# Attention with head mixing and an expert layer on one core: plain float32 products in place of hi/lo splits, and steps of two mixing blocks

## The chip, the core and the metric

One core of one Trainium2 chip runs the whole kernel in one launch. The metric is the device time of an execution in microseconds (us); lower is better. The core's engines are TensorE (PE, with its weight loads listed apart as PEld), VectorE (DVE), ScalarE (ACT), GpSimd (POOL) and SyncE (SP, which here only issues DMAs).

## What is computed

The inputs are `q`, `k`, `v` of shape (8, 12, 448, 64), that is batch, heads, positions and head size, two 12x12 head-mixing matrices and the weights of 8 experts. All are float32.

```python
scores = (1/8) * q @ k.T                                   # per batch and head: 448 x 448
scores = einsum('bhij,hg->bgij', scores, w_pre)            # first mixing, over heads
attn   = exp(scores - max); attn /= sum(attn) + 1e-9       # over keys j
attn   = einsum('bhij,hg->bgij', attn, w_post)             # second mixing, over heads
x      = (attn @ v) laid out as 3584 tokens x 768
expert = argmax(x @ w_gate); gate = softmax weight of it
out    = gate * (relu(x @ w1[expert]) @ w2[expert])
```

## The kernel before

**Tiles and blocks.** For each batch the 448 queries are cut into four tiles `T` of 120, 120, 120 and 88 queries, 32 tiles in all. A tile is cut into *blocks* of 10 queries; 10 queries x 12 heads fill 120 partitions, so both mixings are matrix products with a block-diagonal 120x120 matrix. There are 12 blocks in a tile of 120 queries and 9 in one of 88: 360 blocks.

**The work of a tile and of a block.** `qk(T, h)` (L196 to L210) makes the scores of one head into a PSUM bank `bs`; ACT copies them to `si` (L208), queries on partitions. `relayout` (L212) is a DMA on SP's queue that brings the rows of one block from `si` to `sb`, with (query, head) on partitions. `split` (L218) makes two float32r numbers of each element on DVE: `sh` by a cast (L223) and the rest `sl` by a subtraction (L224). `mix` (L227) is three float32r products WH·sh + WL·sh + WH·sl into a PSUM bank `bm` (L231 to L233), then the row maximum on DVE (L235), the exponential with its row sum on ACT (L237), two small DVE instructions for the reciprocal (L239, L241), and on DVE the second mixing's matrix scaled by it, `wp` (L243). `post` (L247) is the second mixing: four float32 products, one for each 112 keys, that take the exponentials `et` as weights, so the result comes out with keys on partitions (`bp`, L256); ACT copies it to `pt` (L258). `av` (L263, one pair of heads) is the product with `v` in float32: the even head writes PSUM partitions 0 to 63 and the odd head 64 to 127 (L271). `rows` (L289) turns the tile and adds the expert logits; `dispatch` ranks the tokens and scatters them from POOL's queue (L334).

**Splits of q and k.** A float32r score product has K = 128: partitions 0 to 63 hold the high part of `q` and 64 to 127 the rest. It is multiplied with the high part of `k` (`ka`, L203) and with its rest (`kb`, L204); `k` and `q` are each loaded twice, once per half of the partitions (L89, L109), and split by ACT (L96, L116) and DVE (L97, L117) in float32r.

**Order.** The lists of steps (the loop after `PL, QLEAD, RLEAD, SLEAD = 3, 17, 5, 2`) name what is recorded in step `u`, one step per block: the mix of block `u`, one head's scores of a later tile, the relayout of block `u + 5`, the split of block `u + 2`, an `av` pair, the second mixing of block `u - 3`. A scheduler turns these into a fixed instruction order per engine; from then on each engine runs its list in order. Buffers come from pools: two for `si`, four for `sb`, two raw ones and six pairs of halves for `k`, and one for `v`, whose next batch is loaded by the last `av` of a batch. The experts (L427 on) start when the last tile's tokens are dispatched.

Of the kernel before, what the change touches and what calls it, by code (L numbers as in the profile page):

```python
# [38 lines left out]
def attn_moe_kernel(ctx, tc, qT, kT, v, w_pre, w_post, w_gate, w1, w2, out):  # L39
# [32 lines left out]
    bank_s = [ps_s.tile([P, 512], F32, name=f"bs{n}") for n in range(2)]  # L72
    bank_m = [ps_m.tile([IT, 512], F32, name=f"bm{n}") for n in range(2)]
    bank_p = [ps_p.tile([JC, 512], F32, name=f"bp{n}") for n in range(2)]
    bank_a = ps_a.tile([P, 3, IT], F32, name="ba")
    bank_x = [ps_x.tile([P, 512], F32, name="bx"), bank_s[0]]
    turn = {"s": 0, "m": 0, "p": 0}

    def bank(k, banks):
        turn[k] += 1  # L80
        return banks[turn[k] % len(banks)]

    KK, QQ, VV, SI, SB, SH, EE, PT, XT, KR = ({} for _ in range(10))

    def dma_k(b, c, pool):
        raw = pool.tile([P, KC, S], F32, name="kraw")
        src = kT[b, c * KC:(c + 1) * KC].rearrange("h d j -> d h j")
        for half in range(2):
            nc.sync.dma_start(out=raw[half * D:(half + 1) * D], in_=src)  # L89
        KR[b, c] = raw  # L90

    def split_k(b, c, eng=None):
        raw = KR.pop((b, c))
        ka = k_p.tile([P, KC, S], F32R, name="ka")
        kb = k_p.tile([P, KC, S], F32R, name="kb")
        nc.scalar.copy(out=ka, in_=raw)  # L96
        (eng or nc.vector).tensor_sub(out=kb, in0=raw, in1=ka.bitcast(F32))  # L97
        KK[b, c] = (ka, kb)

    def load_k(b, c):  # L100
        dma_k(b, c, kraw_p)
        split_k(b, c)

    def dma_q(T):
        b, it, ni, _ = geom[T]
        raw = q_p.tile([P, H, IT], F32, name="qraw")
        src = qT[b, :, H * it * IT:H * (it * IT + ni)].rearrange("d (h i) -> d h i", h=H)
        for half in range(2):
            nc.sync.dma_start(out=raw[half * D:(half + 1) * D, :, :ni], in_=src)  # L109
        KR[T] = raw  # L110

    def split_q(T):
        b, it, ni, _ = geom[T]
        raw = KR.pop(T)
        qs = q_p.tile([P, H, IT], F32R, name="qs", bufs=2)
        nc.scalar.copy(out=qs[:, :, :ni], in_=raw[:, :, :ni])  # L116
        nc.vector.tensor_sub(out=qs[D:P, :, :ni], in0=raw[D:P, :, :ni],  # L117
                             in1=qs[D:P, :, :ni].bitcast(F32))
        QQ[T] = qs

    def load_q(T):
        dma_q(T)
        split_q(T)

    def load_v(b):
        vt = v_p.tile([JC, NJ, HD], F32, name="vt")
        nc.sync.dma_start(out=vt, in_=v[b].rearrange("(c p) f -> p c f", p=JC))
        VV[b] = vt

    w12 = const.tile([IT, 2, H], F32, name="w12")  # L130
    for n, w in enumerate((w_pre, w_post)):
        nc.scalar.dma_start(out=w12[:, n, :], in_=w.unsqueeze(0).to_broadcast([IB, H, H]))
# [3 lines left out]
    first = ExitStack()  # L136
    first_p = first.enter_context(tc.tile_pool(name="kfirst", bufs=H // KC))
    dma_q(0)
    for c in range(H // KC):
        dma_k(0, c, first_p)  # L140

# [4 lines left out]
    # mask[p, i] = 1 where p // 12 == i  # L146
    mask = const.tile([IT, IB], F32, name="mask")
    nc.gpsimd.memset(mask, 1.0)
    nc.gpsimd.affine_select(out=mask, in_=mask, pattern=[[-H, IB]], compare_op=ALU.is_ge,
                            fill=0.0, base=0, channel_multiplier=1)  # L150
    nc.gpsimd.affine_select(out=mask, in_=mask, pattern=[[H, IB]], compare_op=ALU.is_ge,
                            fill=0.0, base=H - 1, channel_multiplier=-1)
    Wraw = const.tile([IT, IB, H], F32, name="Wraw")
    WH = const.tile([IT, IT], F32R, name="WH")
    WL = const.tile([IT, IT], F32R, name="WL")
    Wpost = const.tile([IT, H, IB], F32, name="Wpost")
    # SCALE is a power of two: exact
    nc.vector.scalar_tensor_tensor(out=Wraw, in0=w12[:, 0:1, :].to_broadcast([IT, IB, H]),
                                   scalar=SCALE, in1=mask.unsqueeze(2).to_broadcast([IT, IB, H]),
                                   op0=ALU.mult, op1=ALU.mult)  # L160
    nc.vector.tensor_tensor(out=Wpost, in0=w12[:, 1, :].unsqueeze(2).to_broadcast([IT, H, IB]),
                            in1=mask.unsqueeze(1).to_broadcast([IT, H, IB]), op=ALU.mult)
    Wraw = Wraw.rearrange("p i g -> p (i g)")
# [8 lines left out]
    tri = const.tile([P, P], BF16, name="tri")      # tri[m, n] = 1 where m < n  # L172
# [14 lines left out]
    # rows that no token has taken: a token id out of range, gate 0  # L187
# [8 lines left out]
    def qk(T, h):  # L196
        b, it, ni, _ = geom[T]
        if h == 0:
# [6 lines left out]
        if T == 0 and h % 3 == 2:  # L205
            nc.vector.tensor_copy(out=SI[T][:ni, h, :], in_=ps[:ni, :S])
        else:
            nc.scalar.copy(out=SI[T][:ni, h, :], in_=ps[:ni, :S])  # L208
        if it == 3 and b + 1 < B and h % KC == KC - 1:
            load_k(b + 1, h // KC)  # L210

    def relayout(T, s):  # L212
        nb = geom[T][3][s]
        sb = sb_p.tile([IT, S], F32, name="sb")
        nc.sync.dma_start(out=sb[:nb * H], in_=SI[T][s * IB:s * IB + nb])
        SB[T, s] = sb

    def split(T, s):  # L218
        R = geom[T][3][s] * H
        sb = SB.pop((T, s))  # L220
        sh = sh_p.tile([IT, S], F32R, name="sh")
        sl = sh_p.tile([IT, S], F32R, name="sl")
        nc.vector.tensor_copy(out=sh[:R], in_=sb[:R])  # L223
        nc.vector.tensor_sub(out=sl[:R], in0=sb[:R], in1=sh[:R].bitcast(F32))  # L224
        SH[T, s] = (sh, sl)

    def mix(T, s):  # L227
        R = geom[T][3][s] * H
        sh, sl = SH.pop((T, s))
        pm = bank("m", bank_m)  # L230
        nc.tensor.matmul(out=pm[:R, :S], lhsT=WH[:R, :R], rhs=sh[:R], start=True, stop=False)  # L231
        nc.tensor.matmul(out=pm[:R, :S], lhsT=WL[:R, :R], rhs=sh[:R], start=False, stop=False)  # L232
        nc.tensor.matmul(out=pm[:R, :S], lhsT=WH[:R, :R], rhs=sl[:R], start=False, stop=True)  # L233
        st = sm_p.tile([IT, 4], F32, name="st")
        nc.vector.reduce_max(out=st[:R, 0:1], in_=pm[:R, :S], axis=AX.X, negate=True)  # L235
        et = e_p.tile([IT, S], F32, name="et")
        nc.scalar.activation(out=et[:R], in_=pm[:R, :S], func=AF.Exp, bias=st[:R, 0:1],  # L237
                             scale=1.0, accum_out=st[:R, 1:2])
# [433 lines left out]
```

## Time and profile before

| | |
|---|---|
| time, median of 3 runs | 1741.92 us (1730.40 to 1745.09) |
| profiled execution, first to last instruction (span) | 1726.5 us |
| attention up to the last tokens' dispatch | about 0 to 1154 us of the span |
| experts | about 1176 us to the end |
| PE / DVE / ACT / POOL busy | 89% / 61% / 52% / 6% of the span |
| DMA moved | 219.58 MB |

The profiled execution has no other time of its own than the span; it lies 3.9 us under the fastest timed run and 15.4 us under the median. PE's busy time holds the tail of a product that is already overlapped by the next one, so the distance between two starts, not the duration of one, is what a product costs in a dense stretch.

### The profile page before, as it was taken

How to read it: one execution, taken by the hardware profiler on the slowest of the kernel's cores; microseconds unless marked ns; L12 is line 12 of the kernel's file. 1: busy time of each engine (PE TensorE's matmuls, PEld its weight loads, DVE VectorE, ACT ScalarE, POOL GpSimd, SP SyncE). 2: the span in 40 equal slices, each digit the busy share in tenths (PEclk: the TensorE clock that was granted, in tenths of full speed). 3: DMA queues.
4: the chain of work that ended last, by engine and by line, in shares of the span. 5: the costliest groups of instructions: out<-in, count | busy, mean ns of one | idle time of the engine just before them, and what ended most of it. 6: DMA issues, size and time to landing. Idle time of an engine off the chain costs nothing. (4 is left out here: it accounts for less than half of the span.)

```text
span 1726.5 us, 30276 instructions
## 1 busy us (share of the span) xinstructions
PE 1541.7 (89%) x11032; PEld 1341.1 (78%) x11032; DVE 1055.8 (61%) x3159; ACT 903.9 (52%) x1940; POOL 109.3 (6%) x119
## 2 busy tenths in 40 slices
PE   5878978987988988998898898968999999999996
PEld 3667867876876877786787787758898988898986
DVE  4677857876877777786786787753433425335330
ACT  4566756765766656675775676633422314224220
POOL 1000000000000000000000000010110201101000
PEclk9999988999999989998998999988999999999998
DMA  8666656666556666665665655634514326145210
GB/s 180 129 134 129 127 117 137 116 134 140 118 126 148 121 137 128 130 126 129 134 117 128 133 110 114 154 70 162 195 67 165 142 78 215 66 153 210 74 62 34
DMA packets 112169, 219.58 MB, mean 127 GB/s; under 512 B 28226, under 2 KB 83538, under 8 KB 112004
## 3 DMA queue, kind: packets, MB, share of 16 engines
q1 hardware_dynamic: 104896, 193.53, 48.3%
q0 software_dynamic: 6064, 23.86, 3.7%
q8 instruction: 98, 1.61, 0.4%
q14 instruction: 67, 0.55, 0.1%
q10 hardware_dynamic: 1044, 0.04, 0.0%
HBM read 118.03 MB, written 23.06 MB: 82 GB/s over the span
## 5 line engine op out<-in xcount | busy, mean ns | idle before, releaser
L256 PE MATMUL bp<-wp,et 120*112 120x120 f32 (+1 forms) x2880 | 386.1, 276 | 4.2 <-ACT pt L258 2.7
L256 PEld LDWEIGHTS bp<-wp,et 120*112 120x112 f32 (+1 forms) x2880 | 346.7, 180 | 45.4 <-issue 21.4
L258 ACT COPY pt<-bp 112x480 f32<-112x480 f32 x360 | 204.3, 568 | 143.1 <-PE bp L256 142.2
L208 ACT COPY si<-bs 120x448 f32<-120x448 f32 (+1 forms) x380 | 200.8, 531 | 140.4 <-PE bs L204 108.0
L271 PE MATMUL ba<-pt,vt 112*64 112x120 f32 (+1 forms) x3072 | 210.7, 276 | 50.1 <-DMA vt<-in_v 40.7
L237 ACT ACTIVATE et<-bm,st 120x448 f32<-120x448 f32 x360 | 229.5, 638 | 43.2 <-DVE st L235 34.9
L271 PEld LDWEIGHTS ba<-pt,vt 112*64 112x64 f32 x3072 | 162.6, 142 | 110.7 <-issue 95.5
L235 DVE TENSOR_REDUCE st<-bm 120x1 f32<-120x448 f32 x360 | 220.9, 614 | 12.4 <-PE bm L233 12.1
L224 DVE TENSOR_TENSOR sl<-sb,sh 120x448 fp32r<-120x448 f32 x360 | 220.5, 615 | 0.3
L223 DVE CAST sh<-sb 120x448 fp32r<-120x448 f32 x360 | 140.0, 389 | 101.6 <-PE bm L232 51.3
L203 PE MATMUL bs<-ka,qs 128*120 128x448 f32 (+1 forms) x384 | 153.7, 400 | 48.0 <-ACT si L208 33.1
L231 PE MATMUL bm<-sh,WH 120*120 120x448 f32 x360 | 167.6, 465 | 7.6 <-DVE sh L223 4.7
L204 PE MATMUL bs<-kb,qs 128*120 128x448 f32 (+1 forms) x384 | 148.5, 387 | 0.6 <-DVE kb L97 0.6
L500 PE MATMUL pm_h<-xh,ah 128*128 128x512 f32 (+1 forms) x384 | 146.9, 383 | 2.2 <-PEq L552 0.8
L500 PE MATMUL pm_h<-xl,ah 128*128 128x512 f32 (+1 forms) x384 | 146.4, 381 | 0.0
L500 PE MATMUL pm_h<-xh,al 128*128 128x512 f32 (+1 forms) x384 | 146.4, 381 | 0.0
L233 PE MATMUL bm<-sl,WH 120*120 120x448 f32 x360 | 137.6, 382 | 0.2 <-DVE sl L224 0.2
L232 PE MATMUL bm<-sh,WL 120*120 120x448 f32 x360 | 137.5, 382 | 0.0
L519 PE MATMUL pm_y<-bh,hh 128*128 128x384 f32 x480 | 127.9, 343 | 0.0
L504 DVE SCALAR_TENSOR_TENSOR hl<-pm_h,hh 128x512 fp32r<-128x512 f32 (+1 forms) x64 | 42.0, 656 | 136.3 <-ACT hh L503 136.3
L203 PEld LDWEIGHTS bs<-ka,qs 128*120 128x120 f32 (+1 forms) x384 | 72.6, 189 | 67.0 <-ACT si L208 39.9
L519 PE MATMUL pm_y<-bl,hh 128*128 128x384 f32 x480 | 123.6, 336 | 0.0
(106 smaller groups left out, 2177.4 us busy)
## 6 DMA issues: line engine op xcount, KB each, us to landing
sb<-si SPq DMA_DIRECT2D x352, 210.0 KB
wraw<-in_w SPq DMA_DIRECT2D x48, 512.0 KB
wraw<-in_w SPq DMA_DIRECT2D x64, 384.0 KB
kraw<-in_kT SPq DMA_DIRECT2D x96, 224.0 KB
qraw<-in_qT SPq DMA_DIRECT2D x48, 360.0 KB
vt<-in_v SPq DMA_DIRECT2D x8, 1344.0 KB
XD<-xr SPq DMA_DIRECT2D x24, 360.0 KB
qraw<-in_qT SPq DMA_DIRECT2D x16, 264.0 KB
```

What stands on the lines that cost most here:

```text
L203: nc.tensor.matmul(out=ps[:ni, :S], lhsT=qs, rhs=ka[:, h % KC, :], start=True, stop=False)
L204: nc.tensor.matmul(out=ps[:ni, :S], lhsT=qs, rhs=kb[:, h % KC, :], start=False, stop=True)
L208: nc.scalar.copy(out=SI[T][:ni, h, :], in_=ps[:ni, :S])
L224: nc.vector.tensor_sub(out=sl[:R], in0=sb[:R], in1=sh[:R].bitcast(F32))
L231: nc.tensor.matmul(out=pm[:R, :S], lhsT=WH[:R, :R], rhs=sh[:R], start=True, stop=False)
L235: nc.vector.reduce_max(out=st[:R, 0:1], in_=pm[:R, :S], axis=AX.X, negate=True)
L237: nc.scalar.activation(out=et[:R], in_=pm[:R, :S], func=AF.Exp, bias=st[:R, 0:1], scale=1.0, accum_out=st[:R, 1:2])
L256: nc.tensor.matmul(out=ppv[:, c, :], lhsT=et[:R, c * JC:(c + 1) * JC], rhs=wp[:R, :, :nb], start=True, stop=True)
L258: nc.scalar.copy(out=PT[T][:, :, :, s * IB:s * IB + nb].rearrange("p c h i -> p (c h) i"), in_=pp[:, :NJ * R].rearrange("p (x i) -> p x i" ...
L271: nc.tensor.matmul(out=pa[r * D:(r + 1) * D, :ni], lhsT=VV[b][:, c, h * D:(h + 1) * D], rhs=PT[T][:, c, h, :ni], start=(c == 0), stop=(c = ...
L500: nc.tensor.matmul(out=ph[:, :n], lhsT=wx[:, fs], rhs=xx[:, kt, :n], start=(m == 0), stop=(m == 3 * NK1 - 1))
L519: nc.tensor.matmul(out=py[g][:, :384], lhsT=hx[:, kt, ts], rhs=wx[:, g * 384:(g + 1) * 384], start=(n == 0), stop=(n == 3 * NK2 - 1))
```

## The change

Nothing changes in the experts. In the attention:

- Scores: `q` and `k` are loaded once, with the two heads of a pair on partitions 0 to 63 and 64 to 127, and are used as float32 without a split. `qk(T, c)` does a pair: four float32 products with K = 64 and 224 keys each, the even head's into one PSUM bank and the odd head's into another; one ACT copy takes both banks to `si`.
- First mixing: one float32 product with a 124x124 matrix, no split of `sb`.
- A step is two blocks. `mix` fills two banks, one DVE instruction takes both maxima; ACT still does one exponential per block; the small DVE instructions serve both blocks. `wp` is made by GpSimd (L218 of the new kernel). The second mixing follows one step later, always with 120 columns, and DVE instead of ACT copies it to `pt`.
- `sb` is four fixed buffers of two blocks each, rows 4 to 123, cleared once; the relayout is issued two steps ahead. The `k` pool holds two batches, `v` has two buffers, the next batch's `k` is loaded during the second tile and its `v` in step 8 of a batch. There is no hand-ordered first tile any more. The loads of the first expert's `w1` begin two steps ahead of the last tile instead of one step behind its start.

```diff
-    v_p = att.enter_context(tc.tile_pool(name="vp", bufs=1))
+    v_p = [kq.enter_context(tc.tile_pool(name="vp0", bufs=1, side="right")),
+           att.enter_context(tc.tile_pool(name="vp1", bufs=1))]
     si_p = att.enter_context(tc.tile_pool(name="sip", bufs=2))
...
+    bank_s = ps_s.tile([P, 2, 512], F32, name="bs")
+    bank_m = ps_m.tile([P, 2, 512], F32, name="bm")
...
+    def load_k(b, c):
+        kt = k_p.tile([P, S], F32, name="kt")
+        nc.sync.dma_start(out=kt, in_=kT[b, 2 * c:2 * c + 2].rearrange("h d j -> (h d) j"))
+        KK[b, c] = kt
...
-        ps = bank("s", bank_s)
-        ka, kb = KK[b, h // KC]
-        qs = QQ[T][:, h, :ni]
-        nc.tensor.matmul(out=ps[:ni, :S], lhsT=qs, rhs=ka[:, h % KC, :], start=True, stop=False)
-        nc.tensor.matmul(out=ps[:ni, :S], lhsT=qs, rhs=kb[:, h % KC, :], start=False, stop=True)
...
+        for n in range(2):
+            ns = slice(n * S // 2, (n + 1) * S // 2)
+            for r in range(2):
+                hs = slice(r * D, (r + 1) * D)
+                nc.tensor.matmul(out=bank_s[:ni, r, ns], lhsT=qt[hs, c, :ni], rhs=kt[hs, ns],
+                                 start=True, stop=True)
+        nc.scalar.copy(out=SI[T][:ni, 2 * c:2 * c + 2, :], in_=bank_s[:ni, :, :S])
+        if it == 1 and b + 1 < B:
+            load_k(b + 1, c)
...
+        for c in range(nh):
+            nc.tensor.matmul(out=bank_m[:R1, c, :S], lhsT=Wpre[:R1, :], rhs=sb[:R1, c, :],
+                             start=True, stop=True)
+        nc.vector.reduce_max(out=st[:R1, 0, :nh], in_=bank_m[:R1, :nh, :S], axis=AX.X, negate=True)
+        for c in range(nh):
+            nc.scalar.activation(out=et[:R1, c, :], in_=bank_m[:R1, c, :S], func=AF.Exp,
+                                 bias=st[:R1, 0, c:c + 1], scale=1.0,
+                                 accum_out=st[:R1, 1, c:c + 1])
...
+            nc.gpsimd.tensor_scalar(out=wp[:R1, c, :], in0=Wpost[:R1], scalar1=st[:R1, 2, c:c + 1],
+                                    scalar2=None, op0=ALU.mult)
...
+                nc.tensor.matmul(out=pp[:, c * IT:(c + 1) * IT],
+                                 lhsT=et[:R1, n, c * JC:(c + 1) * JC],
+                                 rhs=wp[:R1, n, :], start=True, stop=True)
...
+            nc.vector.tensor_copy(
+                out=PT[T][:, :, :, i0:i0 + nq].rearrange("p c h i -> p (c h) i"),
+                in_=bank_p[n][:, :NJ * IT].rearrange("p (x i) -> p x i", i=IB)[:, :, :nq])
...
-        if pr == NPAIR - 1 and it == 3 and b + 1 < B:
-            load_v(b + 1)
...
-    PL, QLEAD, RLEAD, SLEAD = 3, 17, 5, 2
+    PL, QLEAD, RLEAD = 1, 8, 2
...
+        if it == 0 and b + 1 < B:
+            at(u0 + 8, 2, load_v, b + 1)
+        for c in range(NPAIR):
+            at(max(u0 - QLEAD + c * 5 // 6, -1), 3, qk, T, c)
```

What the scheduler makes of it, on PE in steady state (names: `bm` first mixing, `bs` scores, `ba` product with v, `bp` second mixing). Before, two blocks:

```order
L231 MATMUL bm_107<-sh,WH 120x448
L232 MATMUL bm_107<-sh,WL 120x448
L233 MATMUL bm_107<-sl,WH 120x448
L203 MATMUL bs_104<-ka,qs 120x448
L204 MATMUL bs_104<-kb,qs 120x448
L271 MATMUL ba<-pt,vt 64x120 x8
L256 MATMUL bp_108<-wp,et 112x120 x4
L231 MATMUL bm_106<-sh,WH 120x448
L232 MATMUL bm_106<-sh,WL 120x448
L233 MATMUL bm_106<-sl,WH 120x448
L203 MATMUL bs_105<-ka,qs 120x448
L204 MATMUL bs_105<-kb,qs 120x448
```

After, two steps (four blocks):

```order
L206 MATMUL bm<-sb_152,Wpre 124x448 x2
L182 MATMUL bs<-kt,qt 120x224 x4
L248 MATMUL ba<-pt,vt 64x120 x8
L229 MATMUL bp_109<-wp,et 112x120 x4
L229 MATMUL bp_110<-wp,et 112x120 x4
L206 MATMUL bm<-sb_149,Wpre 124x448 x2
L182 MATMUL bs<-kt,qt 120x224 x4
L229 MATMUL bp_109<-wp,et 112x120 x4
L229 MATMUL bp_110<-wp,et 112x120 x4
```

Six float32r products of 448 columns have become two float32 ones of 448 (L206), and the four score products of 448 columns of two heads have become four of 224 (L182); the second mixing and the product with `v` stand as they were.

On DVE in steady state (`st` holds maxima, sums and reciprocals). Before, two blocks:

```order
L223 CAST sh<-sb 120x448
L235 TENSOR_REDUCE st<-bm_107 120x1
L224 TENSOR_TENSOR sl<-sb,sh 120x448
L239 TENSOR_SCALAR st<-st 120x1
L223 CAST sh<-sb 120x448
L241 RECIPROCAL st<-st 120x1
L235 TENSOR_REDUCE st<-bm_106 120x1
L243 TENSOR_SCALAR wp<-Wpost,st 120x120
L224 TENSOR_TENSOR sl<-sb,sh 120x448
L239 TENSOR_SCALAR st<-st 120x1
L241 RECIPROCAL st<-st 120x1
L243 TENSOR_SCALAR wp<-Wpost,st 120x120
```

After, one step of two blocks:

```order
L208 TENSOR_REDUCE st<-bm 124x2
L252 COPY xt<-ba 128x3x88
L213 TENSOR_SCALAR st<-st 124x2
L215 RECIPROCAL st<-st 124x2
L234 COPY pt<-bp_109 112x48x10
L234 COPY pt<-bp_110 112x48x10
```

The casts and subtractions for `sh` and `sl` and the products for `wp` are gone from DVE, and two copies out of `bp` stand behind the reciprocal instead.

On SP's queue, from the start of the kernel to the first relayouts. Before:

```order
L109 DMA qraw<-in_qT 64x1440 x2
L89 DMA kraw<-in_kT 64x2x448 x12
L109 DMA qraw<-in_qT 64x1440 x2
L127 DMA vt<-in_v 112x4x768
L215 DMA sb<-si 120x1x448 x4
```

After:

```order
L95 DMA qt<-in_qT 64x6x120 x2
L87 DMA kt<-in_kT 128x448 x6
L95 DMA qt<-in_qT 64x6x120 x2
L87 DMA kt<-in_kT 128x448 x3
L100 DMA vt<-in_v 112x4x768
L87 DMA kt<-in_kT 128x448 x3
L100 DMA vt<-in_v 112x4x768
L197 DMA sb_149<-si 120x1x448 x2
```

Ahead of the first relayout stand now four loads of `q` of half the size, twelve of `k` that hold two batches and not one, and `v` of two batches and not of one.

## Rows read from the trace of the kernel before

**Rows 1.** The profile's page, part 1: each engine's busy time in us, its share of the span, and its instructions.

```profile
PE 1541.7 (89%) x11032; PEld 1341.1 (78%) x11032; DVE 1055.8 (61%) x3159; ACT 903.9 (52%) x1940; POOL 109.3 (6%) x119
```

**Rows 2.** Stretches of the span: from and to in us, length, then busy time of PE, PEld, DVE, ACT and POOL with their records, the granted TensorE clock (1.00 is 2.4 GHz), the DMA share and GB/s. First the steady attention whole and two dense stretches in it; then (rows with only PE and PEld) the first product of the mixing, L231, alone in the same three: its count is the number of blocks.

```profile
60.00:1150.00 1090.00, 974.50 (x8101) 832.21 (x8102) 818.32 (x2774) 702.93 (x1616) 32.52 (x31) 0.94 0.60 126
706.00:771.00 65.00, 65.00 (x582) 56.33 (x581) 54.55 (x188) 46.47 (x109) 2.00 (x2) 1.00 0.60 117
...
60.00:1150.00 1090.00, 162.76 (x350) 67.21 (x350) 0.94 0.60 126
706.00:771.00 65.00, 11.27 (x26) 4.56 (x25) 1.00 0.60 117
1063.00:1103.00 40.00, 7.14 (x16) 2.93 (x16) 1.00 0.53 102
```

**Rows 3.** Who waited for whom between 60 and 1150 us: engine, what it waited to start, what it waited for, then us in total, times, and the longest.

```profile
PE ba L271 <- DMA vt<-in_v: 40.7, 7, 6.8
PE bs L203 <- ACT si L208: 30.8, 12, 5.6
PE bx L289 <- DVE xt L275: 28.3, 7, 5.6
ACT ka L96 <- DMA kraw<-in_kT: 52.1, 15, 7.0
ACT si L208 <- DMA sb<-si: 13.3, 7, 4.3
DVE sh L223 <- DMA sb<-si: 31.0, 26, 2.8
```

**Rows 4.** Stretches around one wait for `v`, with the columns of rows 2.

```profile
210.00:216.00 6.00, 4.84 (x37) 4.43 (x35) 5.50 (x24) 4.67 (x15) 0.00 (x0) 1.00 0.76 195
216.00:222.00 6.00, 0.39 (x4) 0.42 (x5) 0.89 (x6) 0.99 (x3) 0.00 (x0) 0.73 0.65 200
222.00:229.00 7.00, 7.00 (x44) 5.35 (x40) 3.48 (x16) 1.73 (x4) 0.99 (x1) 0.50 0.35 68
```

**Rows 5.** PE in order of time in a dense stretch at clock 1.00: start, duration, engine, line, operation, out<-in, weights, moving shape, records. One float32 product leaves two records.

```profile
1063.96 0.44 PE L231 MATMUL bm<-sh,WH 120*120 120x448 f32 x1
...
1064.86 0.37 PE L204 MATMUL bs<-kb,qs 128*120 128x448 f32 x1
1065.07 0.98 PE L256 MATMUL bp<-wp,et 120*112 120x120 f32 x8
1065.82 0.44 PE L231 MATMUL bm<-sh,WH 120*120 120x448 f32 x1
1066.10 0.37 PE L232 MATMUL bm<-sh,WL 120*120 120x448 f32 x1
1066.30 0.37 PE L233 MATMUL bm<-sl,WH 120*120 120x448 f32 x1
1066.51 0.36 PE L203 MATMUL bs<-ka,qs 128*120 128x448 f32 x1
1066.71 0.37 PE L204 MATMUL bs<-kb,qs 128*120 128x448 f32 x1
1067.01 1.04 PE L271 MATMUL ba<-pt,vt 112*64 112x120 f32 x16
1067.98 1.07 PE L256 MATMUL bp<-wp,et 120*112 120x120 f32 x8
1068.81 0.44 PE L231 MATMUL bm<-sh,WH 120*120 120x448 f32 x1
```

**Rows 6.** Groups of instructions by line and shape over the whole span: out<-in, shapes, count | busy us, mean ns of one | idle before it and what ended it.

```profile
L235 DVE TENSOR_REDUCE st<-bm 120x1 f32<-120x448 f32 x352 | 216.0, 614 | 12.2 <-PE bm L233 11.9
L241 DVE RECIPROCAL st<-st 120x1 f32<-120x1 f32 x352 | 55.1, 157 | 3.4
L275 DVE COPY xt<-ba 128x360 f32<-128x360 f32 x48 | 25.2, 526 | 2.3 <-PE ba L271 1.4
L237 ACT ACTIVATE et<-bm,st 120x448 f32<-120x448 f32 x352 | 224.5, 638 | 43.1 <-DVE st L235 34.9 <-DVE lgs L305 2.9 <-DVE st L241 1.2
L237 ACT ACTIVATION_READ_ACCUMULATOR et<-bm,st 120x1 f32 x352 | 69.7, 198 | 0.0
L208 ACT COPY si<-bs 120x448 f32<-120x448 f32 x284 | 150.4, 534 | 122.2 <-PE bs L204 92.2 <-DMA sb<-si 13.3 <-issue 8.9
```

**Rows 7.** Groups on POOL, same columns.

```profile
L334 POOL DMA_INDIRECT TB<-tg,di x32 | 33.5, 1047 | 1116.1 <-DVE wp L243 814.3 <-DVE di L333 294.1 <-DVE nslot L472 7.6
L171 POOL COPY xg<-ident 128x128 f32<-128x128 f32 x6 | 1.5, 283 | 0.0
```

**Rows 8.** DMA issues of the page (what, queue, count, KB each), and from the order of time the first use of a relayout.

```profile
kraw<-in_kT SPq DMA_DIRECT2D x96, 224.0 KB
qraw<-in_qT SPq DMA_DIRECT2D x48, 360.0 KB
vt<-in_v SPq DMA_DIRECT2D x8, 1344.0 KB
...
31.47 0.39 DVE L223 CAST sh<-sb 120x448 fp32r<-120x448 f32 x1 [3.28 <-DMA sb<-si]
```

More of the change, by code (lines that the diff above doesn't have):

```diff
@@ L26 @@
 IB = 10
+NB = 2 * IB
+IQ = 5
+R0, R1 = 4, 124
 JC, NJ = 112, 4
 NPAIR = H // 2
-KC = 2
 CAP = 512
@@ L77, in attn_moe_kernel @@
[L77 to L87, printed above, removed]
-        for half in range(2):
[L89 to L119, printed above, removed]
@@ L121, in load_q @@
-    def load_q(T):
-        dma_q(T)
-        split_q(T)
+    bank_x = [ps_x.tile([P, 512], F32, name="bx"), bank_s[:, 0, :]]
+    KK, QQ, VV, SI, SB, EE, PT, XT = ({} for _ in range(8))
+    def load_k(b, c):
+        kt = k_p.tile([P, S], F32, name="kt")
+        nc.sync.dma_start(out=kt, in_=kT[b, 2 * c:2 * c + 2].rearrange("h d j -> (h d) j"))
+        KK[b, c] = kt
+    def load_q(T):
+        b, it, ni, _ = geom[T]
+        qt = q_p.tile([P, NPAIR, IT], F32, name="qt")
+        src = qT[b, :, H * it * IT:H * (it * IT + ni)].rearrange("d (c t i) -> t d c i", c=NPAIR, t=2)
+        for half in range(2):
+            nc.sync.dma_start(out=qt[half * D:(half + 1) * D, :, :ni], in_=src[half])
+        QQ[T] = qt
@@ L135, in attn_moe_kernel @@
     nc.scalar.activation(out=warm, in_=warm, func=AF.Exp)
[L136 to L140, printed above, removed]
+    load_q(0)
+    for c in range(NPAIR):
+        load_k(0, c)
     ident = const.tile([P, P], F32, name="ident")
     make_identity(nc, ident)
-    mask = const.tile([IT, IB], F32, name="mask")
+    mask = const.tile([P, IB], F32, name="mask")
     nc.gpsimd.memset(mask, 1.0)
@@ L156, in attn_moe_kernel @@
[L156 to L163, printed above, removed]
@@ L168, in attn_moe_kernel @@
+    nc.vector.tensor_tensor(out=Wpost, in0=w12[:, 1, :].unsqueeze(2).to_broadcast([P, H, IB]),
+                            in1=mask.unsqueeze(1).to_broadcast([P, H, IB]), op=ALU.mult)
+    Wpost = Wpost.rearrange("p g i -> p (g i)")
+    sbs = [sb_p.tile([P, 2, S], F32, name=f"sb{n}") for n in range(4)]
+    for t in sbs:
+        nc.gpsimd.memset(t, 0.0)
     xg = const.tile([P, NPAIR, XG], F32, name="xg")
@@ L216, in relayout, with mix @@
+        nc.scalar.copy(out=SI[T][:ni, 2 * c:2 * c + 2, :], in_=bank_s[:ni, :, :S])
+        if it == 1 and b + 1 < B:
+            load_k(b + 1, c)
+    nsb = {"n": 0}
+    def relayout(T, s):
+        sb = sbs[nsb["n"] % len(sbs)]
+        nsb["n"] += 1
+        for c, nq in enumerate(geom[T][3][s]):
+            q0 = s * NB + c * IB
+            nc.sync.dma_start(out=sb[R0:R0 + nq * H, c, :], in_=SI[T][q0:q0 + nq])
         SB[T, s] = sb
-    def split(T, s):
-        R = geom[T][3][s] * H
+    def mix(T, s):
@@ L220, in split @@
         sb = SB.pop((T, s))
[L221 to L238, printed above, removed]
-        nc.vector.tensor_scalar(out=st[:R, 2:3], in0=st[:R, 1:2], scalar1=1e-9, scalar2=None,
-                                op0=ALU.add)
-        nc.vector.reciprocal(out=st[:R, 3:4], in_=st[:R, 2:3])
-        wp = e_p.tile([IT, H, IB], F32, name="wp")
-        nc.vector.tensor_scalar(out=wp[:R], in0=Wpost[:R], scalar1=st[:R, 3:4], scalar2=None,
-                                op0=ALU.mult)
@@ L245, in mix @@
+        nc.vector.tensor_scalar(out=st[:R1, 2, :nh], in0=st[:R1, 1, :nh], scalar1=1e-9,
+                                scalar2=None, op0=ALU.add)
+        nc.vector.reciprocal(out=st[:R1, 2, :nh], in_=st[:R1, 2, :nh])
+        wp = e_p.tile([P, 2, IT], F32, name="wp")
+        for c in range(nh):
+            nc.gpsimd.tensor_scalar(out=wp[:R1, c, :], in0=Wpost[:R1], scalar1=st[:R1, 2, c:c + 1],
+                                    scalar2=None, op0=ALU.mult)
         EE[T, s] = (et, wp)
     def post(T, s):
-        nb = geom[T][3][s]
@@ L392, in attn_moe_kernel @@
         at(ua + 5 * w // NPAIR + 2, 9, dispatch, T)
-    with tc.manual_schedule():
-        split_q(0)
-        split_k(0, 0)
-        split_k(0, 1)
-        for c in range(H // KC):
-            if c + 2 < H // KC:
-                split_k(0, c + 2)
-            for h in range(KC * c, KC * c + KC):
-                qk(0, h)
-    first.close()
-    pt_p = att.enter_context(tc.tile_pool(name="ptp", bufs=2))
-    x_p = att.enter_context(tc.tile_pool(name="xp", bufs=1))
     at(0, 2, load_v, 0)
```

82 lines of the change are left out of this document (37 added, 45 removed).

## Prediction

> **What bounds the kernel now.** I read the busy table first: PE 89%, far ahead of DVE (61%) and ACT (52%) [rows 1]. The experts are not touched, so the question is the attention. The view of stretches shows two speeds there. Between 60 and 1150 us PE starts 350 blocks, 3.11 us each. In the stretches where PE never stops, 706 to 771 and 1063 to 1103, a block takes 65/26 = 40/16 = 2.50 us at granted clock 1.00 [rows 2]. So the attention is bound by PE's own products at 2.50 us a block, and 1090 - 350 x 2.50 = 215 us of the 1090 are something else. PE's idle time is 1090 - 974.5 = 115.5 us of it. The view of waits says where that comes from: products with `v` waiting for the load of `v` (40.7 us in 7 waits), scores waiting for ACT's copy of a score tile (30.8), the token rows waiting for DVE (28.3); and ACT itself stands 52.1 us before raw `k` [rows 3]. The reader should see that these are DMA waits that reach PE through engines that work in order: one load of `v` per batch into one buffer, raw `k` that ACT must split ahead of the next exponential, and a score buffer that is free only when its last relayout has landed (13.3 us). The clock adds to it. Around one wait for `v` PE does 0.39 us of work in 6 us, and the granted clock is 0.50, the 1.2 GHz level, in the 7 us behind it [rows 4]. The mean of 0.94 over the whole stretch [rows 2] means 12%, or 131 us, at half speed; with some 40 of these idle anyway, about 45 us are lost so. Idle and clock make 160 of the 215 us; the other 55 are small gaps that I do not name.
>
> **The change, term by term.** *First mixing on PE.* Before: L231, L232 and L233 take 0.28, 0.20 and 0.21 from start to start [rows 5]; the first of these holds the tail of what precedes it, so three times 0.205 = 0.615 us. After: one float32 product of 448 columns. The float32 rate is that of the second mixing: 8 records of 120 columns from 1067.98 to 1068.81, 0.104 us each, against 0.205 us for 448 float32r columns [rows 5]. That is 0.866 ns a column and record against 0.458. Two records of 448 columns are 0.78 us; four times the float32r product would be 0.82. I take 0.79: +0.175 us a block, **+63 us** over 360 blocks. This term is sure to be a loss: the split costs PE less than plain float32.
>
> *Scores on PE.* Before: 2 x 0.205 per head, 0.82 us a pair, 192 pairs. After: four float32 products of 224 columns, 8 records of 0.194 us, 1.55 us if they run one behind the other and 0.78 if the two heads, on different halves of the array's rows, run side by side. The nearest row is the product with `v`, where two heads lie on different halves of the columns: 16 records of 120 columns would be 1.66 us in a row and take 0.97 [rows 5], so halves do run side by side there. With the start of one record's skew (0.19) the pair is 0.97; I take 1.0, **+35 us**, with ends of -8 (0.78) and +178 (1.75: one behind the other, with 0.2 for two changes of layout).
>
> The change of layout has a price of its own, seen where the product with `v` follows the scores: 0.30 us from L204 to L271 instead of 0.205 [rows 5]. The Trainium skill states the same as a rule (TensorEngine Tiling (Array Packing), Key Properties): "Changing tiling mode (not just tile) drains the TensorE". By that rule every pair of scores would pay on both sides, while by the row a pair that is followed by a product with `v`, which pays already, costs one more at most. The full price is a rival below.
>
> *Second mixing, product with v, token rows.* The same products; +0.
>
> *DVE.* The two splits and `wp` go. What a step of two blocks leaves: one maximum over 896 columns, about 0.614 + 448 x 1 ns = 1.06 us (1 ns a column from L235 and L275: 88 ns for 88 columns), two small ones at 0.16, two copies of 480 columns at 0.526 + 0.12 = 0.65: 2.7 us [rows 6]. *ACT*: two exponentials with their sums, 2 x 0.84, and a pair's copy of 896 columns, 0.95 to 1.07: 2.7 us [rows 6]. PE needs 2 x (2.50 + 0.175 + 0.10) = 5.5 us a step, so both hide under it with half their time to spare.
>
> *Waits that are added.* The bank pair `bm` is single now: the next mix starts after maximum and first exponential, 1.06 + 0.84 = 1.9 us behind the last one; PE has 5.5 - 1.6 = 3.9 us of other products meanwhile (scores, `v`, second mixing). `wp` from GpSimd: two instructions between 0.283 us (a 128x128 copy there) and 1.05 (an indirect DMA's issue) each [rows 7]; I take the copy, the nearest in size. The chain from the mix is 1.06 + 1.68 + 0.32 + 0.57 = 3.6 us, or 5.2 at the upper end. Its user is queued on PE a full step later, behind the next mix, at 5.5 us or more. What stands behind it on PE is the next mix, so the cover is gone from some 5.5 us on; then each further us is paid in each of 184 steps. The scatter, once a tile, takes 1.05 us of POOL's time in the same place.
>
> *DMA.* `k` and `q` are loaded once: half of 96 x 224 KB and of the `q` loads is gone [rows 8]. `v` comes one batch ahead; ACT no longer stands before raw `k`. A relayout has two steps, 11 us, to land. At the start, though, four `q`, twelve `k` and two `v` are queued ahead of the first relayout: 720 + 2688 + 2688 = 6.1 MB against 1.44 + 2.69 + 1.34 = 5.5. Before, the first relayout's data are used at 31.5 us [rows 8]; with 11% more ahead of it, **+3 us**. Here the shorter preparation gains nothing, the queue decides.
>
> **The sum.** Of the 215 us the waits for `v` and raw `k` and the clock behind them have no cause left. The score buffer's wait stays: the first scores of each batch's first tile are queued in the same step as the last relayout of the buffer that they take. I keep 20 us for that, 15 for the clock behind such waits and 20 of what I could not name: 55, so 160 are gained. 160 - 63 - 35 - 3 = 59 us. The span of 1726.5 becomes 1667.5; with the 15.4 us by which the median stands above this span, **1683 us**. This is below a gain of 160 because plain float32 takes back 98 us on the engine that bounds.
>
> **Rivals.** *More is hidden.* Only 25 us of the 215 stay and a pair takes 0.84: 190 - 63 - 4 - 3 = 120 us, 1622. For it: in 706 to 771 PE ran 65 us without a stop even with DVE at 84% [rows 2]. Against: the score buffer's wait is still in the order.
>
> The Trainium skill says that matmuls on different row groups start about 4 ns apart (TensorE: Matmul & The Clock Gate, The mechanism, in its part on packing), which would put a pair near 0.78 us; no row here shows two row halves.
>
> *The drain in full.* A pair costs 0.78 + 0.19 and twice 0.1 to 0.13, 1.2 us: +73 instead of +35, 1721. For it the 0.1 us of rows 5; against it that most pairs are followed by a product with `v`.
>
> *Row halves don't overlap.* Slower: a pair takes 1.55 to 1.75 us, +159 at 1.65, and the gain becomes a loss of 65: 1807. For it: no row shows halves of the rows side by side; both heads write the same PSUM partitions, in two banks, where the product with `v` writes different ones. Against: that product's pairs do overlap. It decides from 1.31 us a pair on, where 160 - 63 - 3 = 94 us are spent.
>
> *Waits come back.* Relayouts queue behind `v` and `k` on the one SP queue, the score buffer's wait grows, and 120 of the 215 us stay: 1742 + 6 = 1748. For it the 31.0 us that DVE waits for relayouts now, with 60% DMA share [rows 2, 3]; against it the 11 us of lead.
>
> **Chances and range.** My forecast 0.50 (own range 1650 to 1710), more hidden 0.15, drain 0.12, waits 0.11, no overlap 0.12. A change of 1% (17 us) is about what a measurement can tell from none. Faster by over 1% (under 1724.5): 0.50 + 0.15 + 0.07 of the drain + 0.02 of the waits = 0.74. Within 1%: 0.05 + 0.06 = 0.11. Slower by over 1%: 0.12 + 0.03 = 0.15. The range goes from 1622 to 1760: it leaves out the case without overlap and half of the deepest gain.
>
> **What would show it.** In the profile after: a dense stretch at 2.75 to 2.8 us a block (5.5 a step); L206 at two records of 448 columns, 0.79 us; a pair of scores (L182) at about 1.0 us from its start to the next line's; no PE wait for `v`; no wait of PE for POOL's `wp`; the granted clock at 0.97 or above between 60 us and the end of the attention; the second mixing's copies on DVE at 0.65 us. Wrong it would be made by L182 at 1.5 us or more, by waits of PE on ACT's score copy over 40 us, or by PE standing idle over 10% of the attention.

## The result and the profile after

The changed kernel takes 1659.59 us (median of 4 runs, 1651.40 to 1661.01) against 1739.24 for the kernel before on the same chip: ratio 0.952, 95% interval 0.948 to 0.957. That is faster by 4.8%, as forecast in kind; the forecast of 1683 is 23 us too high and its range holds the result.

The page's busy line, in answer to [rows 1]: PE nearer to its span, DVE and ACT with less, POOL now at work.

```profile
PE 1562.8 (94%) x11440; PEld 1230.0 (74%) x11440; DVE 791.6 (48%) x1827; ACT 617.7 (37%) x1312; POOL 320.0 (19%) x483
```

Stretches, columns as in [rows 2]: the steady attention, a dense stretch, then both for the mixing product L206 alone (two records are one block), then the attention's end.

```profile
60.00:1000.00 940.00, 921.73 (x7861) 669.68 (x7862) 527.49 (x1365) 400.44 (x946) 216.53 (x355) 1.00 0.58 115
612.00:637.00 25.00, 25.00 (x219) 17.92 (x218) 14.91 (x40) 10.89 (x28) 5.62 (x9) 1.00 0.64 138
...
60.00:1000.00 940.00, 278.33 (x654) 109.74 (x654) 1.00 0.58 115
612.00:637.00 25.00, 7.37 (x18) 2.68 (x16) 1.00 0.64 138
...
1050.00:1100.00 50.00, 27.72 (x278) 21.58 (x276) 23.68 (x89) 10.77 (x27) 13.55 (x17) 0.77 0.28 84
```

327 blocks in 940 us are 2.875 us each, against 3.11. Dense, it is 25/9 = 2.78 (nine blocks only, so good to about 0.1; e5 below confirms it over 327) against the 2.50 that the prediction read. PE is idle for 18 us of the 940, and the granted clock is 1.00, the 2.4 GHz level, where the mean was 0.94. So a block costs more on PE and almost nothing stands between blocks.

PE in order of time, as in [rows 5].

```profile
616.17 1.67 PE L206 MATMUL bm<-sb,Wpre 124*124 124x448 f32 x4
617.77 0.99 PE L182 MATMUL bs<-kt,qt 64*88 64x224 f32 x8
618.70 1.89 PE L229 MATMUL bp<-wp,et 124*112 124x120 f32 x16
620.43 0.86 PE L264 MATMUL bx<-xg,xt 128*120 128x136 f32 x6
621.12 1.67 PE L206 MATMUL bm<-sb,Wpre 124*124 124x448 f32 x4
```

From start to start the mixing takes 1.60 us for two blocks, a pair of scores 0.93 in this tile of 88 queries; in a tile of 120 it takes 0.95, as the rows of e10 below show.

Waits between 60 and 1000 us, as in [rows 3]; no row with `v` is left.

```profile
PE bs L182 <- ACT si L184: 18.0, 29, 2.5
ACT si L184 <- DMA sb<-si: 4.2, 2, 2.1
```

The largest wait of PE is a step that holds two score pairs: the second stands behind ACT's copy of the first, 0.6 us, once a tile. Groups of DVE and POOL, as in [rows 6, 7].

```profile
L234 DVE COPY pt<-bp 112x480 f32<-112x480 f32 x352 | 229.6, 654 | 125.6 <-PE bp L229 121.2 <-PE bx L292 3.6
L218 POOL TENSOR_SCALAR wp<-Wpost,st 124x120 f32<-124x120 f32 x360 | 207.2, 586 | 772.9 <-DVE st L215 723.7 <-PE bm L206 21.6 <-DVE lg L267 12.7
L208 DVE TENSOR_REDUCE st<-bm 124x2 f32<-124x896 f32 x176 | 191.9, 1090 | 144.9 <-PE bm L206 138.8 <-POOL wp L218 5.9 <-issue 0.2
```

### The profile page after: what moved, and what is told of

Its sections match the earlier page's. It is cut to its first block, busy times and chain, and to the rows that moved or that the text cites. A ratio compares the mean times of both kernels' runs of the same rounds, so it can differ in the third digit from the quotient of the medians.

```text
span 1657.2 us, 29537 instructions
## 1 busy us (share of the span) xinstructions
PE 1562.8 (94%) x11440; PEld 1230.0 (74%) x11440; DVE 791.6 (48%) x1827; ACT 617.7 (37%) x1312; POOL 320.0 (19%) x483
## 5 line engine op out<-in xcount | busy, mean ns | idle before, releaser
L210 ACT ACTIVATE et<-bm,st 124x448 f32<-124x448 f32 x360 | 225.2, 630 | 475.2 <-DVE st L208 417.8
L218 POOL TENSOR_SCALAR wp<-Wpost,st 124x120 f32<-124x120 f32 x360 | 207.2, 586 | 772.9 <-DVE st L215 723.7
L229 PE MATMUL bp<-wp,et 124*112 124x120 f32 x2880 | 348.6, 273 | 0.6 <-POOL wp L218 0.4
L229 PEld LDWEIGHTS bp<-wp,et 124*112 124x112 f32 x2880 | 309.6, 177 | 41.1 <-issue 33.8
L206 PE MATMUL bm<-sb,Wpre 124*124 124x448 f32 x720 | 310.7, 553 | 8.3 <-ACT et L210 8.0
L234 DVE COPY pt<-bp 112x480 f32<-112x480 f32 x360 | 234.0, 652 | 131.6 <-PE bp L229 127.1
L208 DVE TENSOR_REDUCE st<-bm 124x2 f32<-124x896 f32 (+1 forms) x184 | 196.9, 1070 | 145.6 <-PE bm L206 138.8
L182 PEld LDWEIGHTS bs<-kt,qt 64*120 64x120 f32 (+1 forms) x1536 | 126.8, 179 | 150.6 <-issue 97.8
L182 PE MATMUL bs<-kt,qt 64*120 64x224 f32 (+1 forms) x1536 | 203.6, 384 | 34.3 <-ACT si L184 28.2
L184 ACT COPY si<-bs 120x896 f32<-120x896 f32 (+1 forms) x192 | 172.9, 901 | 61.1 <-PE bs L182 51.7
L206 PEld LDWEIGHTS bm<-sb,Wpre 124*124 124x124 f32 x720 | 121.7, 189 | 81.4 <-issue 64.9
L467 ACT ACTIVATE hh<-pm_h 128x512 fp32r<-128x512 f32 (+1 forms) x64 | 36.6, 571 | 165.3 <-PE pm_h L464 165.2
```

The source lines that it names most:

```text
L182: nc.tensor.matmul(out=bank_s[:ni, r, ns], lhsT=qt[hs, c, :ni], rhs=kt[hs, ns], start=True, stop=True)
L184: nc.scalar.copy(out=SI[T][:ni, 2 * c:2 * c + 2, :], in_=bank_s[:ni, :, :S])
L206: nc.tensor.matmul(out=bank_m[:R1, c, :S], lhsT=Wpre[:R1, :], rhs=sb[:R1, c, :], start=True, stop=True)
L208: nc.vector.reduce_max(out=st[:R1, 0, :nh], in_=bank_m[:R1, :nh, :S], axis=AX.X, negate=True)
L210: nc.scalar.activation(out=et[:R1, c, :], in_=bank_m[:R1, c, :S], func=AF.Exp, bias=st[:R1, 0, c:c + 1], scale=1.0, accum_out=st[:R1, 1, c ...
L218: nc.gpsimd.tensor_scalar(out=wp[:R1, c, :], in0=Wpost[:R1], scalar1=st[:R1, 2, c:c + 1], scalar2=None, op0=ALU.mult)
```

## The experiments

All ratios are to the kernel before, run beside each; the changed kernel's is 0.952, and 1% is 17 us.

**Scores: is it the row halves?** e2 changes only the order of the four products, e5 the partitions of the odd head (its scores are then the even head's).

```diff
-        for n in range(2):            # e2: even, even, odd, odd
-            for r in range(2):
+        for r in range(2):
+            for n in range(2):
...
-                hs = slice(r * D, (r + 1) * D)
+                hs = slice(0, D)      # e5
```

> The changed kernel with the four score products of a pair in another order: both key halves of the even head, then both of the odd head, instead of the two heads in turn. Theory (a pair takes 0.93 us because the two heads' row halves run side by side): only the inner two products can still overlap, so 8 records of 0.194 us become 6 in a row, 1.16 us, or 1.55 if none overlap: +0.23 to +0.62 us in each of 192 pairs, 44 to 119 us slower, 1703 to 1779. Rival (a product with K = 64 is simply as quick as that, whatever its neighbour): no change, 1660 within 5.

> The changed kernel with all four score products of a pair on partitions 0 to 63, so both heads lie in one half of the array's rows; the odd head's scores are left out of the computation, the even head's stand in both places. Same instructions, same shapes, same data moved. Theory (the pair takes 0.93 us because records of the two heads run side by side in the two row halves): 8 records one behind the other, 8 x 0.183 + 0.1 = 1.56 us, +0.63 us x 192 = 121 us slower than the changed kernel, about 1780. Rival (a float32 product with K = 64 is as quick alone): 1660 within 5.

Measured: e2 0.956 (0.952 to 0.960), 1662.9 us, as the changed kernel; e5 1.051 (1.046 to 1.056), 1834.8 us. PE in e5, a pair in a tile of 120 queries, and then its stretch from 60 to 1100 us, whole and for L206 alone:

```profile
622.10 1.77 PE L182 MATMUL bs<-kt,qt 64*120 64x224 f32 x8
623.80 1.07 PE L229 MATMUL bp<-wp,et 124*112 124x120 f32 x8
...
60.00:1100.00 1040.00, 1040.00 (x7780) 779.85 (x7780) 525.72 (x1358) 399.11 (x940) 215.75 (x356) 1.00 0.53 103
60.00:1100.00 1040.00, 276.56 (x654) 109.28 (x654) 1.00 0.53 103
```

1.70 us a pair instead of 0.95. The experts' first product comes at 1227.1 us instead of 1100.3: 127 us later, where 121 were expected; 14 of them stand already ahead of the first mixing (44.9 us instead of 30.7). (The rest of e5's loss is in the experts, whose token counts change with the scores.) PE never stops in e5: 1040/327 = 3.18 us a block, and less 0.75 us for each of 192 pairs, 0.40 a block, that is 2.78, the dense price of the changed kernel. So K = 64 alone is not quick; the two row halves working side by side save it. Then e2 should have lost, and did not: its theory was wrong in that only neighbours in the order can overlap. Two narrow windows on L182 just where a pair starts, first e2, then e5 (the count in brackets is of records, of PE and then of its weight loads):

```profile
615.28:615.30 0.02, 0.01 (x1) 0.01 (x1) 1.00 0.86 90
615.30:615.33 0.03, 0.03 (x2) 0.03 (x2) 1.00 1.29 119
```

```profile
616.09:616.12 0.03, 0.02 (x1) 0.02 (x1) 1.00 0.90 179
616.12:616.30 0.18, 0.18 (x1) 0.18 (x2) 1.00 0.57 100
```

In e2's program all 192 pairs stand in the order even, even, odd, odd. Still a second record runs within 0.04 us of the first, and the eight records of the pair start two by two, 0.013 us apart, every 0.19 to 0.27 us (in the changed kernel 0.007 us apart). In e5, where all eight lie on one half, the first runs alone and each next one starts at least 0.19 us later. So of two records that start together one must be odd: PE starts an odd product in the idle half ahead of an even one that stands before it in the order.

**v late again, in the changed kernel.** One `v` buffer, loaded by the last product with `v` of a batch, as before.

```diff
+        if pr == NPAIR - 1 and it == 3 and b + 1 < B:
+            load_v(b + 1)
...
-            at(u0 + 8, 2, load_v, b + 1)
```

> The changed kernel with v as it was before: one buffer, the next batch loaded behind the last product with v of a batch. Theory (the load of v was the largest single wait that the change took away): 7 waits of 5 to 7 us on PE come back, 35 to 45 us, with 5 to 20 us at the lower clock behind them: 40 to 65 us slower than the changed kernel, 1700 to 1725. Rival (the waits at a batch's change have several causes in line, and with v late PE only waits where it would wait for relayouts or scores anyway): less than 15 us slower, under 1675.

Measured: 0.977 (0.973 to 0.981), 1700.1 us, 40 us slower than the changed kernel: the theory, at its lower end. Its wait and its stretch (compare 1.00 above):

```profile
PE ba L247 <- DMA vt<-in_v: 31.8, 7, 6.5
```

```profile
60.00:1000.00 940.00, 895.68 (x7524) 653.50 (x7522) 504.36 (x1311) 383.08 (x906) 206.62 (x340) 0.98 0.56 111
```

**The same waits taken out of the kernel before.** e7 loads `v` in six tiles, each as soon as its last reader is done; e8 also loads raw `k` two pairs ahead; e12 adds the float32 first mixing to e8, so that DVE has no split.

```diff
+        if it == 3 and b + 1 < B:      # in av: e7
+            load_vp(b + 1, pr)
...
+            if h == 0:                 # in qk: e8
+                dma_k(b + 1, 0, kraw_p)
+                dma_k(b + 1, 1, kraw_p)
...
+        nc.tensor.matmul(out=pm[:R, :S], lhsT=Wraw[:R, :R], rhs=sb[:R], start=True, stop=True)  # e12
```

> The kernel before with v in six tiles, one for each pair of heads, each loaded for the next batch as soon as the last product of this batch has read it, instead of one load behind the last of them. Theory (the wait for v is 40.7 us of PE and 10 to 25 us of lower clock behind it): 40 to 65 us faster than before, 1672 to 1697. Rival (at a batch's change other transfers are late as well, so v's wait is only replaced): less than 15 us faster.

> The kernel before with v by pairs as in e7_b_v_pairs, and raw k loaded two pairs ahead of its split instead of in the same step. Theory (ACT's 52.1 us before raw k reach PE as waits for exponentials and score copies): another 15 to 40 us, 1640 to 1675. Rival (ACT has half its time free, its wait is off PE's path): within 8 us of e7_b_v_pairs.

> The kernel of e8_b_vk (before, with v by pairs and k early) with one float32 product as first mixing, straight from sb (six buffers), and no casts or subtractions on DVE; scores by heads in float32r, steps of one block and wp on DVE as before. Theory (of the 215 us of excess in the kernel before, what is left behind v and k hangs on the splits that wait for relayouts in DVE's order): PE pays 0.19 us a block, +65, and gets back 40 to 60 us, so it ends 5 to 25 us above e8_b_vk, 1710 to 1730. Rival (the excess has to do with score banks and steps of one block, not with the splits): the full 65 us, 1760 to 1775.

Measured: e7 0.985 (0.981 to 0.989), 26 us faster than before where 40 to 65 were expected; e8 0.975 (0.970 to 0.980), 43 us, which is 11 us under e7 by the medians and 17 by the ratios, between its rival (8) and its theory (15 to 40); e12 0.998 (0.996 to 1.001), so the float32 mixing loses 39 us again, between its theory (5 to 25) and its rival (65). The waits between 60 and 1150 us of e7, e8 and e12, to be read against [rows 3], where the same waits are 30.8 and 13.3:

```profile
ACT si L213 <- DMA sb<-si: 29.1, 9, 4.4
PE bs L208 <- ACT si L213: 33.4, 14, 4.5
```

```profile
ACT si L213 <- DMA sb<-si: 41.0, 12, 6.1
PE bs L208 <- ACT si L213: 35.2, 11, 5.3
```

```profile
ACT si L212 <- DMA sb<-si: 76.1, 21, 7.7
PE bs L207 <- ACT si L212: 64.9, 8, 10.2
```

As the waits for `v` and raw `k` go, this one grows: ACT's copy of the scores stands before the buffer's last relayout, 13.3 us before, then 29.1, 41.0 and 76.1. PE behind it waits hardly more in e7 and e8, and twice as long in e12. What e12 does take away with DVE's splits is PE's wait of the token rows for DVE: 28.3 us before, 22.6 in e8 and none in e12; ACT's wait for raw `k`, down to 11.1 us in e8, is back at 46.5 there. By the lists of steps that relayout is issued in the very step before the tile's first scores, and behind a tile of 9 blocks two steps after them (block u0 - 9 - 6 against u0 - 17). So `v` and `k` alone are worth 43 us in the kernel before, and `v` alone 40 in the changed kernel, where little stands behind it.

**wp on DVE.** `nc.gpsimd.tensor_scalar` becomes `nc.vector.tensor_scalar` in L218.

> The changed kernel with wp made by DVE instead of GpSimd. Theory (PE takes wp a full step after its mix, so where it is made costs nothing; DVE has half its time free): the same within 5 us, 1655 to 1665. Rival (taking wp from DVE is a part of the gain: two more instructions of about 0.2 us stand ahead of the copies of bp and the next maximum): 15 us or more slower, 1675 up. Other way round, if GpSimd's 2 x 0.59 us are late somewhere: up to 10 us faster.

Measured: 0.951 (0.947 to 0.956), the same. DVE takes 278 ns for one where POOL took 586; between 60 and 1000 us PE waits for neither.

**The split mixing in the changed kernel.** In e1 DVE makes `sh` and the rest for a step of two blocks, three float32r products a block follow, ACT copies `pt`, and the relayout is issued three steps ahead. In e6 it is four, and the recorded order of a step is kept. e9 fixes the whole order by hand with the float32 mixing (and with two separate banks and the other changes that its expectation names), e10 the same with the split, e11 moves the scores of a batch's first tile.

```diff
+            for n, (x, y) in enumerate(((WH, sh), (WL, sh), (WH, sl))):       # e10, e11; e1 and e6 into bank_m[:R1, c, :S]
+                nc.tensor.matmul(out=bank_m[c][:R1, :S], lhsT=x[:R1, :], rhs=y[:R1, c, :],
+                                 start=n == 0, stop=n == 2)
...
+    with tc.manual_schedule():                                               # e9, e10, e11
...
-    PL, QLEAD, RLEAD = 1, 8, 2
+    PL, QLEAD, RLEAD = 1, 9, 4
```

> The changed kernel with the first mixing split again: DVE makes a float32r part and a rest of sb (896 columns a step), three float32r products a block take the place of the one float32 product, and ACT again copies the second mixing to pt. Theory (PE alone bounds the attention, float32 mixing costs it 0.80 us a block against 3 x 0.205 = 0.615): about 0.185 us x 350 blocks = 60 to 66 us faster than the changed kernel, 1594 to 1600 us. Rival (the change gained because DVE and ACT lost work; DVE goes back to about 4.5 us of a 5 us step with the splits, or 3.2 without the copies, ACT to 3.9): the waits come back and the time is the same or up to 30 us longer, 1660 to 1690.

> The split first mixing of e1_split_mix once more, with the recorded order of each step kept, so that DVE takes the maximum ahead of the next step's cast and subtraction, the reciprocal behind them, and the relayout is issued four steps ahead instead of three. Theory (e1_split_mix was slow because a cast that waited for its relayout stood ahead of the maximum on DVE; PE itself is cheaper by 0.3 us a step): the step falls to about 5.2 us, 40 to 60 us faster than the changed kernel, 1600 to 1620. Rival (maximum and two exponentials before the single pair of mixing banks is free again are the bound as soon as PE has less to do): no faster than the changed kernel, 1650 to 1690.

> The changed kernel with its float32 mixing, in an order fixed by hand: one score pair a step (begun nine steps ahead), relayouts four steps ahead, the two maxima as two instructions, the rank of the tokens in two steps, the first expert's w1 loaded two steps ahead of its split. Theory (the 28 us of PE behind the copy of a score pair, the waits for w1 and the waits once a tile are all that is left beside PE's own work): 10 to 25 us faster than the changed kernel, 1635 to 1650. Rival (the scheduler's order was hiding more than it lost): 1660 to 1680.

> The kernel of e9_plain_order with the first mixing split as in e1_split_mix. Theory (e1_split_mix and e6_split_hand lost their gain to waits once a tile, of the mixing banks for the exponentials; PE itself needs 1.39 us a step for the six float32r products against 1.60 for the two float32 ones): 0.21 x 184 = 39 us faster than e9_plain_order, up to 0.37 x 184 = 68 if the change of type costs nothing, 1570 to 1610. Rival (DVE and ACT at 4 of less than 5 us a step can't keep up in order, and idle gaps pull the clock down): no faster than e9_plain_order.

> The kernel of e10_split_order with the scores of each batch's first tile begun one step later (eight steps ahead, one step with two pairs), and those of the second tile of the run begun in step 0. Theory (in e10_split_order the copy of a score pair waits 12 times, 56 us in all and up to 7.6, for the last relayout of the buffer that it takes, and PE 34 us behind it): that wait falls to under 20 us and some clock comes back, 15 to 35 us faster than e10_split_order, 1610 to 1630. Rival (relayouts land late because of the load on the queue, whatever the step): within 8 us of it.

Measured: e1 0.972 (0.969 to 0.976), 1691.8 us, 32 us slower than the changed kernel: the rival, at its far end. DVE in one step of e1, where a cast that waits for its relayout stands ahead of the maximum for which ACT and PE wait, and all that PE waits for behind ACT between 60 and 1040 us:

```profile
614.20 0.63 DVE L210 CAST sh<-sb 124x896 fp32r<-124x896 f32 x1 [1.48 <-DMA sb<-si]
614.75 1.09 DVE L224 TENSOR_REDUCE st<-bm 124x2 f32<-124x896 f32 x1
...
PE bs L187 <- ACT si L189: 41.8, 15, 3.7
PE bm L222 <- ACT et L226: 18.4, 21, 2.0
```

So the cast is one link of the chain to the exponentials; PE's larger wait in e1 is for ACT's copy of the scores, and that the cast causes it is not shown. e6 0.961 (0.957 to 0.965), 1677.6: better than e1, again the rival's side. The same waits in e6, where the one for the exponentials comes once a tile, and the clock around one of these (it ends at 646.7 us):

```profile
PE bm L222 <- ACT et L226: 50.9, 29, 2.1
PE bs L187 <- ACT si L189: 2.8, 3, 1.0
```

```profile
644.00:648.00 4.00, 2.26 (x14) 1.46 (x13) 2.96 (x5) 1.39 (x5) 1.26 (x4) 1.00 0.70 109
648.00:652.00 4.00, 3.09 (x22) 2.44 (x24) 0.00 (x0) 1.76 (x2) 0.49 (x1) 0.57 0.56 99
```

PE stood idle for 1.7 us up to 646.7 and for 0.9 up to 648.9; from 648 to 652 us the granted clock is 0.57, near the 1.2 GHz level. e9 0.958 (0.954 to 0.963), 1668.3 us: no faster than the changed kernel, its rival; PE waits as long behind ACT's copy of the scores as before (24.5 us, against 20.2 in the changed kernel). e10 0.943 (0.939 to 0.947), 1643.1 us, is faster than both: 25 us under e9, of 39 to 68 expected. e11 0.949 (0.945 to 0.952) gains nothing over e10: ACT's wait for the score buffer fell (from 56.3 to 30.7 us), but 19.4 us came in that the profile puts down to the load of `k`, and PE's wait behind the copy stayed (34.2 and 36.6). What holds that wait in e10 is open. PE in e10:

```profile
702.97 1.89 PE L252 MATMUL bp<-wp,et 124*112 124x120 f32 x16
704.63 0.45 PE L222 MATMUL bm<-sh,WH 124*124 124x448 f32 x1
704.92 0.36 PE L222 MATMUL bm<-sh,WL 124*124 124x448 f32 x1
...
705.73 0.37 PE L222 MATMUL bm<-sb,WH 124*124 124x448 f32 x1
706.03 1.02 PE L187 MATMUL bs<-kt,qt 64*120 64x224 f32 x8
706.98 1.89 PE L252 MATMUL bp<-wp,et 124*112 124x120 f32 x16
708.71 0.86 PE L287 MATMUL bx<-xg,xt 128*88 128x136 f32 x6
709.32 0.45 PE L222 MATMUL bm<-sh,WH 124*124 124x448 f32 x1
```

The same step that takes 4.95 us in the changed kernel (616.17 to 621.12, with a pair of 88 queries) takes 4.69 (704.63 to 709.32, with one of 120): 0.26 us for two blocks, 0.28 with equal pairs, some 50 us over 360.

## Why the prediction was right, and where it was off

- **The bound.** PE's own products bound the attention before and after: 98% busy after, and moving `wp` between POOL and DVE (e4) moves nothing. Dense 2.78 us a block, forecast 2.75 to 2.8. The price before was read too low, though: the stretches of [rows 2] are short, and one of the 26 products between 706 and 771 us had begun ahead of them. In a longer stretch PE, busy throughout, starts 29 blocks (the whole first, then L231 alone):

```profile
978.00:1052.00 74.00, 74.00 (x649) 1.00 0.61 121
978.00:1052.00 74.00, 12.96 (x29) 5.29 (x29) 1.00 0.61 121
```

  That is 2.55 us, and 2.60 from the first of these starts (978.10) to the last (1050.86). So the products cost 0.18 to 0.23 us a block more, 63 to 80 us over 350 blocks where 98 were forecast, and the excess before was 180 to 197 us, not 215.
- **First mixing, +63 us.** Measured some 50. The old price was right: the first product's longer start, 0.29 in e10, is the tail of what precedes it, for the second mixing ahead of it takes 1.66 us (702.97 to 704.63) where it takes 1.73 ahead of a float32 product. The new one was too high: second and first mixing together take 3.06 us for two blocks in e10 (702.97 to 706.03) and 1.73 + 1.60 = 3.33 in the changed kernel, 0.14 a block against the 0.175 taken. Records of L206 start 0.38 us apart, 0.75 a block and not 0.79; the rest of the 1.60 is 0.09 at the last of them, where the array's layout changes, and the last product of e10's mixing pays that too (0.30 from 705.73 instead of 0.205). By the medians e10 is 25 us under e9.
- **Scores, +35.** A pair is 0.95, forecast 1.0, but the forecast's parts were not the right ones, so that it comes near is in part luck. The skew of 0.19 is not there (the two halves start 0.007 us apart), and the change of layout, for which this sum took 0.03 at most, is: e5's four records more are 0.75 us, 0.19 each, and 0.95 - 4 x 0.19 leaves 0.2 us for both ends of a pair, 0.1 each as in [rows 5]. The rival "no overlap" was real, as e5 shows, but not the case. The rival "drain in full" had the price of the change right, and is too dear at 1.2 us because it adds the skew. The Trainium skill has the rule that a change of tiling mode drains the engine (TensorEngine Tiling (Array Packing), Key Properties); the trace agrees, with these 0.2 us a pair. The Trainium skill also has it that products on different row groups start nearly together (TensorE: Matmul & The Clock Gate, The mechanism); the traces agree, with 0.007 us in the changed kernel and 0.013 in e2.
- **Waits, 160 of 215 gained.** Right in sum, not in cause. The excess was 180 to 197 us, as said above; 55 were to stay, and (2.875 - 2.78) x 327 = 31 us are left between 60 and 1000, so 150 to 165 are gained. But `v` and `k`, named as the chief causes, give 43 us when taken from the kernel before. Of the rest, the score buffer's wait is the largest that e8 still shows; the forecast let it stay at 20 us, and after, ACT waits 4.2 us for it. That this part went with the splits, the steps of two blocks or the shorter leads together was read from waits; no run isolates it, and e12 shows that taking away DVE's splits alone does not do it.
- **wp on GpSimd.** 586 ns instead of the 283 taken; hidden as forecast (e4).
- **The start, +3.** The first mixing starts at 30.74 us; before, the first relayout was used at 31.47 [rows 8]. No loss where 3 us were forecast.
- **Not foreseen: the end.** The first expert's `w1` is now split while the last tiles run, and ACT stands before it ahead of the exponentials. ACT and PE from 1015 to 1050 us:

```profile
ACT ah L329 <- DMA wraw<-in_w: 13.3, 4, 6.0
PE bm L206 <- ACT et L210: 6.3, 4, 3.0
```

In e9, which issues these loads two steps ahead of the split, PE is busy for all of the 40 us from 1000 to 1040, here for 33.9. The way from the last tokens' scatter to the experts' first product takes 25.2 us against 21.4, and the experts 556.9 against 550.8; the latter may be scatter, for with the same instructions they take 556.0 and 558.2 in e7 and e8. With PE's 6.3 us of wait some 16 us are lost here. In the span: (3.114 - 2.875) x 350 = 84 gained, 1 at the start, less 16 is 69; measured 1726.5 - 1657.2 = 69.3, where 59 were forecast. The other 13 us of the miss are the 15.4 that were added to come from the span to a median; after, median and span lie 2.4 apart.

## What to carry to other kernels

Waits that stand one behind the other on in-order engines are not worth their listed times: take one out and look which grows. A cheaper product pays only if the rest keeps up with it: the split mixing lost 32 us in one order and won 16 in another (e1 and e10, 3% apart, with the further changes of e10), about as much as the split saves on PE. Four float32 products with K = 64 took 0.95 us on both halves of the rows against 1.70 on one, whatever order they were written in. And the price of a dense stretch is taken from start to start over a long one: the windows of 40 and 65 us read it up to 0.1 us a block too low here.

## What the runs showed of the hardware

Float32 with K = 64 on one row half: 1.70 us for eight records of 224 columns; on both halves 0.95, even if the two products of a half stand next to each other in the order, because PE starts the other half's product ahead of them (e2). A pair holds 0.2 us beyond its four times 0.19: the two changes of the array's layout. GpSimd takes 586 ns for a 124x120 scaling, DVE 278. Behind a gap of 1.7 us on PE (up to 646.7 us), and with another of 0.9 (up to 648.9), the granted clock was 0.57 from 648 to 652 us (e6).
